# The head of a fused attention and mixture kernel: another written order, whole-tile conversions, more instructions ahead of the first scores

## The chip, the cores and the metric

The kernel runs on one core of a Trainium2 chip (trn2). The metric is the device time of one execution in microseconds (us). Engines are named as the profile names them: PE is TensorE, PEld its weight loads, DVE is VectorE, ACT is ScalarE, POOL is GpSimd, SP is SyncE, which issues the loads and stores.

## The reference

Three layers follow one another on 4 x 576 = 2304 tokens of width 512 (8 heads of 64). The first is attention, where a row sees only keys at a small distance (a window of 32 for heads 0 to 3; every fourth key of 128 for heads 4 to 7). The second is a gated layer, the third a mixture of 8 experts with 4 slots each.

```python
scores = np.where(masks, (q @ k.T) / np.sqrt(64), -1e9)
attn = np.exp(scores - scores.max(-1)); attn /= attn.sum(-1) + 1e-9
x = attn @ v                                     # 2304 x 512
x = (sigmoid(x @ w_gate) * (x @ w_val)) @ w_out  # 512 -> 1536 -> 512
logits = x @ phi                                 # 512 -> 32 slots
slot_input = softmax(logits, axis=0).T @ x       # 8 experts x 4 slots
slot_out[e] = relu(slot_input[e] @ w1[e]) @ w2[e]   # 512 -> 1024 -> 512
out = softmax(logits, axis=1) @ slot_out
```

## The kernel before

Tokens are worked on in five blocks: four of 512 and one of 256. In each block the 8 heads make four pairs, taken in the order `HP_ORDER`; a pair of a block is a *unit*. A unit passes these steps, each a function of the kernel:

- `scores`: on PE, two matmuls that add the mask (L146), then 32 products of q and k (L160), in fp32, which the trace lists as 64 matmuls and 64 weight loads. The result is in two PSUM tiles `s_ps`.
- `soft_max`: two maxima (L174) and two subtractions (L177) on DVE. `soft_exp`: ACT (L186). `soft_sum`: sum, a scalar addition, reciprocal on DVE (L191 to L193). `soft_norm`: the product with the reciprocal, on DVE or POOL (L197).
- `turn_unit`: four transposes on PE (L209), and a copy by ACT into `pt_ring` (L210).
- `sums` (by `weighted`, L236): 32 products of the turned probabilities and v, again 64 matmuls and 64 loads in the trace.
- `finish_unit`: the result is split into `x_hi` (ACT, L264) and `x_lo` (the difference, DVE, L265), so that a matmul in a faster format keeps precision.

The gated layer's first matmul (L485, `l1_chunk`) takes for each weight half and each unit three products: high weights by `x_hi`, high weights by `x_lo`, low weights by `x_hi`. The weights come in as 64-bit numbers in a tile `st` (`wd` in HBM). `convert_begin` orders that load; `convert_top` (ACT, L370), `convert_shift` and `convert_low` (DVE, L374 and L378) and `convert_sum` (POOL, L382) make 32-bit floats of them in `fw`, in two halves of 512 columns; `split_half` makes the high part `whl` (ACT, L442) and the low part (DVE, L443). `convert_end` notes the result to be stored.

`first_block` is the head of the program: the four units of the first block, the conversion of the weights z = 0 and z = 1, and the first L485 matmuls (`chunk`, six for each unit). Within it, `kept`, `kp` and `at` fix the order on each engine to the written one; behind it, a scheduler chooses. `keep_warm(n)` is n dummy matmuls on zeros (L110, 128 x 512, one weight load each), `pad_stream` is `PAD` short fp32 matmuls on data that is there (L873). `WARM` is the count of dummy matmuls at the start. `first_qk` and `first_v` order the loads of the second block, whose first instruction on PE is a mask matmul (L146). The lines of `first_block` from the second unit's exponentials to the fourth unit's turn are those that the change reorders.

Of the kernel before, what the change touches and what calls it, by code (L numbers as in the profile page):

```python
# [9 lines left out]
U32 = mybir.dt.uint32  # L10
# [16 lines left out]
WARM = 3  # L27
PAD = 8
# [24 lines left out]
def tile_kernel(  # L53
# [54 lines left out]
    def keep_warm(count):  # L108
        for _ in range(count):
            kept(nc.tensor.matmul(idle, lhsT=zero[:, 0:P], rhs=zero[:, 512:1024], start=True, stop=True))  # L110

    keep_warm(WARM)

# [71 lines left out]
    def soft_exp(u):  # L185
        kp(nc.scalar.activation(u["s"], u["s"], AF.Exp, scale=0.125))  # L186
# [172 lines left out]
    def convert_begin(z):  # L359
        i = n_conv[0]  # L360
        n_conv[0] += 1
        stage(z)
        if i + 1 < len(turn):
            stage(turn[i + 1])
        store()
        return b8(("ws", "ws", "gb", "xt")[i % 4] if i < NF else ("gb", "xt")[i % 2], [P, 2, 1024], F32, "fw")

    def convert_top(z, fw, h):
        c = slice(512 * h, 512 * h + 512)
        kp(nc.scalar.activation(fw[:, 0, c], staged[z][:, c, 1].bitcast(F32), AF.Prelu, scale=2.0**-112, alpha=2.0**32))  # L370

    def convert_shift(fw, h):
        top = fw[:, 0, 512 * h : 512 * h + 512].bitcast(U32)
        kp(nc.vector.tensor_scalar(top, top, 3, None, ALU.logical_shift_left))  # L374

    def convert_low(z, fw, h):
        c = slice(512 * h, 512 * h + 512)
        kp(nc.vector.tensor_scalar(fw[:, 1, c].bitcast(I32), staged[z][:, c, 0], 2.0**-29, None, ALU.mult))  # L378

    def convert_sum(fw, h):  # L380
        top, low = (fw[:, r, 512 * h : 512 * h + 512].bitcast(I32) for r in range(2))
        kp(nc.gpsimd.tensor_tensor(low, top, low, ALU.add))  # L382
# [10 lines left out]
    def convert(z):  # L393
        fw = convert_begin(z)
        for h in range(2):
            convert_top(z, fw, h)
            convert_shift(fw, h)
            convert_low(z, fw, h)
            convert_sum(fw, h)
        return convert_end(z, fw)  # L400
# [487 lines left out]
    def first_block():  # L888
# [10 lines left out]
        fw = [None, None]  # L899
        fw[0] = convert_begin(0)  # L900
# [9 lines left out]
        soft_norm(u[0], nc.gpsimd)  # L910
        scores(u[2], range(4))
        soft_max(u[2])
        soft_exp(u[2])
        soft_sum(u[1])
        soft_norm(u[1], nc.gpsimd)
        keep_warm(4)
        convert_top(0, fw[0], 0)
        turn_unit(u[0])
        convert_top(0, fw[0], 1)
        soft_sum(u[2])  # L920
        convert_low(0, fw[0], 0)
        convert_shift(fw[0], 0)
        convert_sum(fw[0], 0)
        soft_norm(u[2], nc.vector)
        convert_low(0, fw[0], 1)
        convert_shift(fw[0], 1)
        convert_sum(fw[0], 1)
        keep_warm(5)
        scores(u[3], range(4))
        turn_unit(u[1])  # L930
        soft_max(u[3])
        sums(u[0], u[2])
        finish_unit(u[0])
        soft_exp(u[3])
        whl = new_w()
        split_half(whl, fw[0][:, 1], 0, nc.vector)
        turn_unit(u[2])
        soft_sum(u[3])
        soft_norm(u[3], nc.vector)
        split_half(whl, fw[0][:, 1], 1, nc.vector)  # L940
        sums(u[1], u[3])
        finish_unit(u[1])
        convert_end(0, fw[0])
        first_qk()
        fw[1] = convert_begin(1)
        first_v()
        g = l1_tile(0, 0)
# [7 lines left out]
        turn_unit(u[3])  # L955
        for h in range(2):
            convert_top(1, fw[1], h)
            convert_low(1, fw[1], h)
            convert_shift(fw[1], h)
            convert_sum(fw[1], h)  # L960
        sums(u[2])
        finish_unit(u[2])
        chunk(HP_ORDER[1])
        sums(u[3])
        pad_stream(u[3])
        finish_unit(u[3])
        chunk(HP_ORDER[2])
        whl1 = new_w()
        for h in range(2):
            split_half(whl1, fw[1][:, 1], h, nc.vector)  # L970
        convert_end(1, fw[1])
# [508 lines left out]
```

## Time and profile before

| | before |
|---|---|
| median of three runs | 487.08 us (485.86 to 487.42) |
| the profiled execution's own time | 485.42 us |
| its span, first to last instruction | 483.6 us |
| PE busy | 463.6 us, 96% of the span |
| DVE, ACT, POOL busy | 308.4, 212.7, 156.8 us |
| instructions in the span | 12700 |

The profile is of one execution. A view by windows gives the busy time of each engine in a stretch and the clock granted to PE, where 1.00 is full speed; a timeline lists consecutive instructions of one kind with start and duration, and in brackets the idle time before them and what ended it. "issue" there means that nothing in the profile explains the wait. Since matmuls overlap, the start of the next instruction is often a better measure of a matmul than its duration.

### The profile page before, as it was taken

Reading aid. Unit: us, or ns where it says so; the run is one execution under the profiler, and the core shown is the slowest. Engines: PE = TensorE matmul, PEld = TensorE weight load, DVE = VectorE, ACT = ScalarE, POOL = GpSimd, SP = SyncE. Lnnn points to the kernel's source line nnn. Section 1 sums busy time; section 2 is a strip of 40 time slices with the busy share of each in tenths; the row PEclk is TensorE's granted clock in tenths of the full one; section 3 lists DMA queues with packets and bytes.
Section 4 is the critical chain, followed back from the end, with each engine's and each line's share of the span. In section 5 each row is a group of like instructions: output and inputs, shape, how many; then the busy total and the mean of one; then the engine's idle time right before and its main releaser. Section 6 shows DMA issues by size and latency. Waiting matters only on the chain.

```text
span 483.6 us, 12700 instructions
## 1 busy us (share of the span) xinstructions
PE 463.6 (96%) x5421; PEld 358.2 (74%) x5425; DVE 308.4 (64%) x627; ACT 212.7 (44%) x413; POOL 156.8 (32%) x134
## 2 busy tenths in 40 slices
PE   6799999999999999999999999999999999999993
PEld 3578877888778787787778888888887889842552
DVE  4877879848678666467776566656547765532623
ACT  2545455544446544445345545554535344300222
POOL 0334454425554663612033242333312124110100
PEclk9899999999999999999999999999999999999998
DMA  8979987986997792122220220211499886689966
GB/s 324 413 294 359 317 277 267 314 341 201 359 341 299 249 362 81 68 89 87 89 87 3 87 87 1 87 35 54 165 372 426 344 332 230 229 323 373 427 243 240
DMA packets 23720, 112.12 MB, mean 232 GB/s; under 512 B 2288, under 2 KB 7152, under 8 KB 14576
## 3 DMA queue, kind: packets, MB, share of 16 engines
q1 hardware_dynamic: 23664, 111.32, 61.8%
q8 instruction: 42, 0.69, 0.5%
q14 instruction: 14, 0.11, 0.1%
HBM read 97.16 MB, written 14.16 MB: 230 GB/s over the span
## 4 chain that ended last, share of the span: by engine, by line
PE 78%; DVE 4%; issue 1%; ACT 1%; POOL 1%; DVEq 0%; ACTq 0%; POOLq 0%
PE l1ps L485 25%; PE pa L610 13%; PE pe L610 7%; PE tp L743 4%; PE so_ps L1309 3%; PE pd L610 3%; PE h_ps L1247 3%; PE s_ps L236 3%; PE sp L768 2%; PE lt_ps L714 2%; PE s_ps L160 2%; PE wt_ps L419 1%; PE tr L209 1%; PE op L1347 1%; DVE whl L443 1%
## 5 line engine op out<-in xcount | busy, mean ns | idle before, releaser
L485 PE MATMUL l1ps<-x_hi,whl 128*128 128x512 f32 x384 | 130.6, 404 | 1.2 <-DVE g L471 1.0
L485 PEld LDWEIGHTS l1ps<-x_hi,whl 128*128 128x128 f32 x384 | 72.6, 189 | 18.1 <-DVE g L471 1.6
L485 PE MATMUL l1ps<-x_lo,whl 128*128 128x512 f32 x192 | 75.7, 394 | 0.0
L382 POOL TENSOR_TENSOR fw<-fw 128x512 int32<-128x512 int32 x36 | 47.8, 1337 | 55.9 <-DVE fw L374 24.7
L485 PEld LDWEIGHTS l1ps<-x_lo,whl 128*128 128x128 f32 x192 | 36.5, 190 | 6.3
L471 DVE SCALAR_TENSOR_TENSOR g<-g,l1ps 128x512 f32<-128x512 f32 (+1 forms) x36 | 21.4, 595 | 24.9 <-PE l1ps L485 24.8
L485 PE MATMUL l1ps<-x,whl 128*128 128x256 f32 x288 | 37.0, 285 | 0.0
L485 PEld LDWEIGHTS l1ps<-x,whl 128*128 128x128 f32 x288 | 35.4, 192 | 0.4 <-ACT whl L442 0.2
L443 POOL TENSOR_TENSOR whl<-w,whl 128x512 fp32r<-128x512 f32 x12 | 15.9, 1329 | 51.2 <-ACT whl L442 39.7
L497 ACT ACTIVATE g<-l1ps 128x512 f32<-128x512 f32 (+1 forms) x36 | 18.9, 526 | 30.3 <-PE l1ps L485 30.3
L443 DVE TENSOR_TENSOR whl<-fw,whl 128x512 fp32r<-128x512 f32 x24 | 21.8, 913 | 11.4 <-ACT whl L442 10.3
L442 ACT CAST whl<-fw 128x512 fp32r<-128x512 f32 x24 | 14.8, 622 | 26.6 <-POOL fw L382 26.5
L743 PEld LDWEIGHTS tp<-cst,g 128*128 128x128 f32 x192 | 21.3, 140 | 5.4 <-issue 4.1
L743 PE MATMUL tp<-cst,g 128*128 128x128 f32 x192 | 25.0, 275 | 0.0
L197 POOL TENSOR_TENSOR sm<-sm,su 128x512 f32<-128x512 f32 x14 | 17.3, 1237 | 23.7 <-DVE su L193 22.0
L370 ACT ACTIVATE fw<-st 128x512 f32<-128x512 f32 x36 | 22.8, 672 | 4.4 <-DMA st<-wd 4.4
L748 ACT COPY gt<-tp 128x512 f32<-128x512 f32 x24 | 14.0, 585 | 24.1 <-PE tp L743 21.4
L443 POOL TENSOR_TENSOR whl<-wst,whl 128x512 fp32r<-128x512 f32 x12 | 16.3, 1357 | 25.6 <-ACT whl L442 20.6
L673 DVE TENSOR_TENSOR tm<-pe,tm 128x512 f32<-128x512 f32 x12 | 8.3, 691 | 24.7 <-PE pe L610 24.7
L374 DVE TENSOR_SCALAR fw<-fw 128x512 uint32<-128x512 uint32 x36 | 20.5, 588 | 3.2 <-ACT fw L370 2.9
L236 PE MATMUL s_ps<-pt_ring,v 64*64 64x32 f32 (+1 forms) x992 | 18.9, 224 | 3.7 <-issue 3.7
L378 DVE TENSOR_SCALAR fw<-st 128x512 int32<-128x512 uint32 x36 | 18.2, 534 | 5.1 <-DMA st<-wd 4.9
(483 smaller groups left out, 954.3 us busy)
## 6 DMA issues: line engine op xcount, KB each, us to landing
ew<-w SPq DMA_DIRECT2D x32, 1024.0 KB, 7.5
st<-wd SPq DMA_DIRECT2D x18, 1024.0 KB, 7.9
wst<-wg SPq DMA_DIRECT2D x12, 1024.0 KB, 6.3
v<-qkv SPq DMA_DIRECT2D x20, 512.0 KB, 6.6
wg<-fw SPq DMA_DIRECT2D x12, 512.0 KB, 6.3
w<-wg SPq DMA_DIRECT2D x6, 1024.0 KB, 6.5
qk<-qkv SPq DMA_DIRECT2D x10, 576.0 KB, 5.1
qk<-qkv SPq DMA_DIRECT2D x8, 528.0 KB, 5.3
```

Of the source, the lines that this page charges most:

```text
L197: kp(norm.tensor_tensor(s, s, u["su"].unsqueeze(2).to_broadcast([P, 8, 64]), ALU.mult))
L236: nc.tensor.matmul(o, lhsT=v[k, t, i, r, :], rhs=p_[k, 2 * r + t, i, 0:nq], start=True, stop=True)
L370: kp(nc.scalar.activation(fw[:, 0, c], staged[z][:, c, 1].bitcast(F32), AF.Prelu, scale=2.0**-112, alpha=2.0**32))
L374: kp(nc.vector.tensor_scalar(top, top, 3, None, ALU.logical_shift_left))
L378: kp(nc.vector.tensor_scalar(fw[:, 1, c].bitcast(I32), staged[z][:, c, 0], 2.0**-29, None, ALU.mult))
L382: kp(nc.gpsimd.tensor_tensor(low, top, low, ALU.add))
L443: kp(eng.tensor_tensor(whl[:, 1, h], src[:, h], whl[:, 0, h].bitcast(F32), ALU.subtract))
L471: return nc.vector.scalar_tensor_tensor(g, g, 1.0, val, ALU.add, ALU.mult)
L485: nc.tensor.matmul(pt, lhsT=whl[:, w_, a, dc, :], rhs=x_[n][:, dc, :], start=(dc == HP_ORDER[0] and (w_, x_) == (0, x_hi)), stop=(dc == HP ...
L497: nc.scalar.activation(g, pt, AF.Tanh, scale=0.5)
L610: nc.tensor.matmul(pt, lhsT=w[:, w_, P * c : P * c + P], rhs=x_[:, c], start=first and c == 0 and w_ == 0 and x_ is hi, stop=c == 1 and w_ ...
L743: nc.tensor.transpose(tp[:, c], g_sb[self.n, 4 * q + c][:, P * j : P * j + P], ident)
```

## The change

It moves lines of `first_block` and changes three numbers:

- `WARM` from 3 to 7, and ahead of those, `SMALL` = 24 dummy matmuls of 32 x 32, each with its load: 28 matmuls and 28 loads more ahead of the first scores. `PAD` from 8 to 3. The dummy matmuls between the third and the fourth scores are 2, 2 and 3, in place of 4 and 5.
- In the head, `convert_top`, `convert_shift` and `convert_low` take the whole tile of 1024 columns at once; `convert_sum` keeps halves. Later conversions are as before.
- The second unit's sum and norm stand ahead of the third scores. The first and the second unit's turn both stand ahead of the fourth scores; before, the second one stood behind them.
- The fourth unit's exponentials, sum and norm stand ahead of `finish_unit` of the first unit; the third unit's turn behind that. The fourth unit's turn and the conversion of z = 1 stand ahead of the first `chunk`; the sums of the third and the fourth unit both stand between the first and the second `chunk`.

```diff
@@ -24,8 +24,9 @@
 HIP = 200
 LA = 2
 WO_AT = (12, 13, 14, 15, 16, 17)
-WARM = 3
-PAD = 8
+WARM = 7
+SMALL = 24
+PAD = 3
 GA = 0
 NRM = True
 ND = 4
@@ -109,6 +110,9 @@
         for _ in range(count):
             kept(nc.tensor.matmul(idle, lhsT=zero[:, 0:P], rhs=zero[:, 512:1024], start=True, stop=True))
 
+    for i in range(SMALL):
+        g = slice(32 * (i % 4), 32 * (i % 4) + 32)
+        kept(nc.tensor.matmul(idle[g, 0:32], lhsT=zero[:, 0:32], rhs=zero[:, 512:544], start=True, stop=True))
     keep_warm(WARM)
 
     def keep_busy(count):
@@ -365,20 +369,21 @@
         store()
         return b8(("ws", "ws", "gb", "xt")[i % 4] if i < NF else ("gb", "xt")[i % 2], [P, 2, 1024], F32, "fw")
 
-    def convert_top(z, fw, h):
-        c = slice(512 * h, 512 * h + 512)
+    HALVES = (slice(0, 512), slice(512, 1024))
+    WHOLE = slice(0, 1024)
+
+    def convert_top(z, fw, c):
         kp(nc.scalar.activation(fw[:, 0, c], staged[z][:, c, 1].bitcast(F32), AF.Prelu, scale=2.0**-112, alpha=2.0**32))
 
-    def convert_shift(fw, h):
-        top = fw[:, 0, 512 * h : 512 * h + 512].bitcast(U32)
+    def convert_shift(fw, c):
+        top = fw[:, 0, c].bitcast(U32)
         kp(nc.vector.tensor_scalar(top, top, 3, None, ALU.logical_shift_left))
 
-    def convert_low(z, fw, h):
-        c = slice(512 * h, 512 * h + 512)
+    def convert_low(z, fw, c):
         kp(nc.vector.tensor_scalar(fw[:, 1, c].bitcast(I32), staged[z][:, c, 0], 2.0**-29, None, ALU.mult))
 
-    def convert_sum(fw, h):
-        top, low = (fw[:, r, 512 * h : 512 * h + 512].bitcast(I32) for r in range(2))
+    def convert_sum(fw, c):
+        top, low = (fw[:, r, c].bitcast(I32) for r in range(2))
         kp(nc.gpsimd.tensor_tensor(low, top, low, ALU.add))
 
     def convert_end(z, fw):
@@ -392,11 +397,11 @@
 
     def convert(z):
         fw = convert_begin(z)
-        for h in range(2):
-            convert_top(z, fw, h)
-            convert_shift(fw, h)
-            convert_low(z, fw, h)
-            convert_sum(fw, h)
+        for c in HALVES:
+            convert_top(z, fw, c)
+            convert_shift(fw, c)
+            convert_low(z, fw, c)
+            convert_sum(fw, c)
         return convert_end(z, fw)
 
     ticks = [0]
@@ -896,8 +901,7 @@
         start_unit(u[3], "gb")
         for z in range(4):
             start_values(u, z)
-        fw = [None, None]
-        fw[0] = convert_begin(0)
+        fw = convert_begin(0)
         scores(u[0], range(4))
         soft_max(u[0])
         soft_exp(u[0])
@@ -908,42 +912,46 @@
         keep_warm(2)
         soft_sum(u[0])
         soft_norm(u[0], nc.gpsimd)
+        soft_sum(u[1])
+        soft_norm(u[1], nc.gpsimd)
+        convert_top(0, fw, WHOLE)
         scores(u[2], range(4))
         soft_max(u[2])
+        keep_warm(2)
+        turn_unit(u[0])
+        keep_warm(2)
+        turn_unit(u[1])
         soft_exp(u[2])
-        soft_sum(u[1])
-        soft_norm(u[1], nc.gpsimd)
-        keep_warm(4)
-        convert_top(0, fw[0], 0)
-        turn_unit(u[0])
-        convert_top(0, fw[0], 1)
+        convert_low(0, fw, WHOLE)
+        convert_shift(fw, WHOLE)
+        for c in HALVES:
+            convert_sum(fw, c)
         soft_sum(u[2])
-        convert_low(0, fw[0], 0)
-        convert_shift(fw[0], 0)
-        convert_sum(fw[0], 0)
         soft_norm(u[2], nc.vector)
-        convert_low(0, fw[0], 1)
-        convert_shift(fw[0], 1)
-        convert_sum(fw[0], 1)
-        keep_warm(5)
+        keep_warm(3)
         scores(u[3], range(4))
-        turn_unit(u[1])
         soft_max(u[3])
         sums(u[0], u[2])
-        finish_unit(u[0])
+        whl = new_w()
+        split_half(whl, fw[:, 1], 0, nc.vector)
         soft_exp(u[3])
-        whl = new_w()
-        split_half(whl, fw[0][:, 1], 0, nc.vector)
-        turn_unit(u[2])
         soft_sum(u[3])
         soft_norm(u[3], nc.vector)
-        split_half(whl, fw[0][:, 1], 1, nc.vector)
+        finish_unit(u[0])
+        turn_unit(u[2])
+        split_half(whl, fw[:, 1], 1, nc.vector)
         sums(u[1], u[3])
         finish_unit(u[1])
-        convert_end(0, fw[0])
+        convert_end(0, fw)
+        turn_unit(u[3])
         first_qk()
-        fw[1] = convert_begin(1)
+        fw = convert_begin(1)
         first_v()
+        convert_top(1, fw, WHOLE)
+        convert_low(1, fw, WHOLE)
+        convert_shift(fw, WHOLE)
+        for c in HALVES:
+            convert_sum(fw, c)
         g = l1_tile(0, 0)
         pt = [ps_l1.tile([P, 512], F32, tag="l1", name="l1ps") for _ in range(2)]
 
@@ -952,23 +960,17 @@
                 l1_chunk(0, whl, a, pt[a], dc)
 
         chunk(HP_ORDER[0])
-        turn_unit(u[3])
-        for h in range(2):
-            convert_top(1, fw[1], h)
-            convert_low(1, fw[1], h)
-            convert_shift(fw[1], h)
-            convert_sum(fw[1], h)
         sums(u[2])
         finish_unit(u[2])
-        chunk(HP_ORDER[1])
         sums(u[3])
         pad_stream(u[3])
         finish_unit(u[3])
+        chunk(HP_ORDER[1])
         chunk(HP_ORDER[2])
         whl1 = new_w()
         for h in range(2):
-            split_half(whl1, fw[1][:, 1], h, nc.vector)
-        convert_end(1, fw[1])
+            split_half(whl1, fw[:, 1], h, nc.vector)
+        convert_end(1, fw)
         chunk(HP_ORDER[3])
         for a in range(2):
             l1_gate(g, a, pt[a])
```

PE between the third scores (rows up to here: `s_ps_211`, `s_ps_212`) and the fourth (`s_ps_286`, `s_ps_287`), before; `idle<-pm` is a dummy matmul, `tr` a turn:

```order
L160 MATMUL s_ps_212<-qk 32x64
L110 LDWEIGHTS pm
L110 MATMUL idle<-pm 128x512
...
L209 MATMUL tr<-cst,sm_97 128x128 x4
...
L146 LDWEIGHTS msk
L146 MATMUL s_ps_286<-msk 128x256
```

The same place of the change, where the third scores are `s_ps_245` and `s_ps_246` and the fourth `s_ps_315` and `s_ps_316`:

```order
L164 MATMUL s_ps_246<-qk 32x64
L111 LDWEIGHTS pm
L111 MATMUL idle<-pm 128x512
...
L213 MATMUL tr<-cst,sm_125 128x128 x4
...
L213 MATMUL tr<-cst,sm_125 128x128 x4
...
L150 LDWEIGHTS msk
L150 MATMUL s_ps_315<-msk 128x256
```

Left out are only more dummy matmuls: four ahead of the turn and five behind it before, and now two, two and three. The second turn has come ahead of the fourth scores.

DVE from the third maxima to the fourth, before (`sm` are the probabilities of all units, `fw` and `st` the weights of z = 0; the L191 shown is the second unit's sum, the third's is left out up to its L193):

```order
L174 TENSOR_REDUCE mx<-s_ps_211 128x4
...
L177 TENSOR_TENSOR sm_97<-s_ps_212,mx 128x256
L191 TENSOR_REDUCE su<-sm_97 128x8
L192 TENSOR_SCALAR su<-su 128x8
...
L193 RECIPROCAL su<-su 128x8
L378 TENSOR_SCALAR fw<-st 128x512
L374 TENSOR_SCALAR fw<-fw 128x512
L197 TENSOR_TENSOR sm_97<-sm_97,su 128x512
L378 TENSOR_SCALAR fw<-st 128x512
L374 TENSOR_SCALAR fw<-fw 128x512
L174 TENSOR_REDUCE mx<-s_ps_286 128x4
```

And of the change, from the second unit's sum on:

```order
L195 TENSOR_REDUCE su<-sm_125 128x8
...
L197 RECIPROCAL su<-su 128x8
L178 TENSOR_REDUCE mx<-s_ps_245 128x4
...
L181 TENSOR_TENSOR sm_125<-s_ps_246,mx 128x256
L383 TENSOR_SCALAR fw<-st 128x1024
L380 TENSOR_SCALAR fw<-fw 128x1024
L195 TENSOR_REDUCE su<-sm_125 128x8
L196 TENSOR_SCALAR su<-su 128x8
L197 RECIPROCAL su<-su 128x8
L201 TENSOR_TENSOR sm_125<-sm_125,su 128x512
L178 TENSOR_REDUCE mx<-s_ps_315 128x4
```

The second unit's sum now stands ahead of the third maxima, and the conversions, each of the whole tile, ahead of the third unit's sum.

DVE from the fourth subtractions to the fourth norm, before (the first unit's `x_lo` is made from `s_ps_211` and `s_ps_212`):

```order
L177 TENSOR_TENSOR sm_97<-s_ps_287,mx 128x256
L265 TENSOR_TENSOR x_lo<-s_ps_211,x_hi 128x2x128
L265 TENSOR_TENSOR x_lo<-s_ps_212,x_hi 128x2x128
L443 TENSOR_TENSOR whl<-fw,whl 128x512
L191 TENSOR_REDUCE su<-sm_97 128x8
...
L193 RECIPROCAL su<-su 128x8
L197 TENSOR_TENSOR sm_97<-sm_97,su 128x512
L443 TENSOR_TENSOR whl<-fw,whl 128x512
L265 TENSOR_TENSOR x_lo<-s_ps_286,x_hi 128x2x128
```

And of the change:

```order
L181 TENSOR_TENSOR sm_125<-s_ps_316,mx 128x256
L448 TENSOR_TENSOR whl<-fw,whl 128x512
L195 TENSOR_REDUCE su<-sm_125 128x8
...
L197 RECIPROCAL su<-su 128x8
L201 TENSOR_TENSOR sm_125<-sm_125,su 128x512
L269 TENSOR_TENSOR x_lo<-s_ps_245,x_hi 128x2x128
L269 TENSOR_TENSOR x_lo<-s_ps_246,x_hi 128x2x128
L448 TENSOR_TENSOR whl<-fw,whl 128x512
L269 TENSOR_TENSOR x_lo<-s_ps_315,x_hi 128x2x128
```

The two differences for the first unit's `x_lo` have gone behind the fourth norm.

## Rows read from the trace of the kernel before

**Rows 1.** Page: span, busy time of each engine, instruction queue (packets, MB, share).
```profile
span 483.6 us, 12700 instructions
...
PE 463.6 (96%) x5421; PEld 358.2 (74%) x5425; DVE 308.4 (64%) x627; ACT 212.7 (44%) x413; POOL 156.8 (32%) x134
...
q8 instruction: 42, 0.69, 0.5%
```

**Rows 2.** Windows: stretch, length, busy us (instructions) by engine, clock, DMA share, GB/s.
```profile
0.00:34.00 34.00, 26.20 (x645) 18.67 (x652) 23.18 (x54) 14.11 (x28) 7.87 (x10) 0.90 0.92 360
```

**Rows 3.** Timeline of PE in the head: start, duration, instruction, idle before.
```profile
1.45 1.46 PE L110 MATMUL idle<-pm 128*128 128x512 bf16 x3 [1.45 <-DVE pm L101]
4.93 0.61 PE L146 MATMUL s_ps<-msk 128*128 128x256 bf16 x2 [2.01 <-DMA msk<-masks]
...
9.77 0.86 PE L160 MATMUL s_ps<-qk 64*32 64x64 f32 x64
...
12.45 0.66 PE L209 MATMUL tr<-cst,sm 128*128 128x128 f32 x4 [0.85 <-POOL sm L197]
...
15.71 1.13 PE L236 MATMUL s_ps<-pt_ring,v 64*64 64x32 f32 x63
19.50 0.19 PE L236 MATMUL s_ps<-pt_ring,v 64*64 64x32 f32 x1 [2.66 <-issue]
19.63 1.10 PE L209 MATMUL tr<-cst,sm 128*128 128x128 f32 x4
...
23.54 1.05 PE L485 MATMUL l1ps<-x_hi,whl 128*128 128x512 f32 x2
...
27.96 0.62 PE L485 MATMUL l1ps<-x_hi,whl 128*128 128x512 f32 x2
...
28.97 1.14 PE L236 MATMUL x_ps<-pt_ring,v 64*64 64x32 f32 x64
30.04 0.31 PE L873 MATMUL pad<-pt_ring,v 128*32 128x8 f32 x16
...
33.14 0.39 PE L146 MATMUL s_ps<-msk 128*128 128x256 bf16 x2
```

**Rows 4.** Windows on both sides of the clock's rise in the head.
```profile
19.83:26.66 6.83, 6.83 (x102) 5.42 (x101) 4.38 (x10) 3.27 (x8) 0.00 (x0) 0.51 1.01 396
26.66:33.10 6.44, 6.44 (x154) 5.20 (x146) 5.35 (x11) 4.08 (x10) 2.68 (x2) 1.00 0.85 322
```

**Rows 5.** Timelines of DVE and POOL (last three rows) in the head.
```profile
14.89 0.37 DVE L378 TENSOR_SCALAR fw<-st 128x512 int32<-128x512 uint32 x1
...
16.12 1.49 DVE L378 TENSOR_SCALAR fw<-st 128x512 int32<-128x512 uint32 x1
...
17.87 0.74 DVE L174 TENSOR_REDUCE mx<-s_ps 128x4 f32<-128x256 f32 x2
18.53 0.74 DVE L177 TENSOR_TENSOR sm<-s_ps,mx 128x256 f32<-128x256 f32 x2
...
21.77 0.68 DVE L191 TENSOR_REDUCE su<-sm 128x8 f32<-128x512 f32 x1
...
22.93 0.69 DVE L197 TENSOR_TENSOR sm<-sm,su 128x512 f32<-128x512 f32 x1
...
11.36 1.04 POOL L197 TENSOR_TENSOR sm<-sm,su 128x512 f32<-128x512 f32 x1 [10.91 <-DVE su L193]
...
15.68 1.65 POOL L382 TENSOR_TENSOR fw<-fw 128x512 int32<-128x512 int32 x1 [0.97 <-DVE fw L374]
18.02 1.26 POOL L382 TENSOR_TENSOR fw<-fw 128x512 int32<-128x512 int32 x1 [0.70 <-DVE fw L374]
```

**Rows 6.** Second hole: PE timeline, then window and instruction queue between the holes.
```profile
135.95 0.62 PE L485 MATMUL l1ps<-x_hi,whl 128*128 128x512 f32 x2
...
143.41 0.59 PE L236 MATMUL s_ps<-pt_ring,v 64*64 64x32 f32 x25 [1.04 <-issue]
...
19.40:143.30 123.90, 121.65 (x1910) 97.46 (x1909) 94.86 (x195) 63.45 (x122) 55.24 (x43) 0.97 0.86 309
...
q8 instruction: 15, 0.25, 0.8%
```

## The prediction

> **What bounds the kernel now.** Page and windows first: PE is busy 463.6 us of 483.6 [rows 1], and 26.20 of the first 34.00 [rows 2]. So 7.8 of its 20.0 idle microseconds lie in the head, and from 34.00 on it works 437.4 of 449.6: later work follows PE's instruction order with hardly a gap, and a microsecond that the head gains or loses moves all that follows. Then the PE timeline of the head [rows 3]. It shows four things. PE has nothing from 2.92 to 4.93, until the masks land (2.01). One matmul before the end of the first sums (x63, x1) it stands 2.66 us, released by "issue", that is by no engine and no data transfer. From 19.83 to 26.66 the granted clock is 0.51, that is 1.2 GHz of 2.4, and 1.00 behind that [rows 4], so two L485 matmuls take 1.05 there and 0.62 later, and a turn (four transposes) 1.10 against 0.66. And the head ends at 33.14, where the mask matmul of the second token block begins.
>
> What the third and fourth unit wait for is read from the VectorE and GpSimd timeline [rows 5]: the maxima of the fourth scores start at 17.87 although PE had those scores behind it when it began the sums at 15.71; VectorE is still converting weights (the low part at 16.12 took 1.49 against 0.37 for the same shape at 14.89, while GpSimd's add ran from 15.68 to 17.33).
>
> Last, the holes with no releaser. A second one, 1.04 us, lies at 143.41, 39 matmuls into a sums stretch [rows 6]. PE and its weight loads count 10846 instructions, the instruction queue 42 packets [rows 1]: 258 to a packet. Between the two holes lie 1910 + 1909 counted instructions and 15 instruction packets [rows 6]: 255 each. I read both holes as PE waiting for its next block of some 256 instructions. Both come at short instructions: a unit's sums are 128 of them (64 loads, 64 matmuls) in 1.13, so a whole block lasts some 2.3 us there.
>
> The Trainium skill (Runtime: NRT & Kernel Launch, Instruction fetch mechanics) has the same picture, blocks of 256 instructions, but calls a crossing "mostly hidden"; by that rule moving a border is worth nothing, which is rival D below. Most crossings here are indeed hidden, these two took 2.66 and 1.04.
>
> **The change, part by part.**
>
> *Start.* Seven first warm matmuls instead of three, and 24 small ones. Three take 1.46 at half clock [rows 3], so four more are some 1.8 (0.43 apart). Small ones: 16 pad matmuls took 0.31 [rows 3], 0.019 each, so 24 are 0.46; at half clock 0.9. Together 2.3 to 2.7 against a gap of 2.01: the first scores start 0.3 to 0.7 later. If the clock rises sooner, the first two units' masks (0.61 against 0.39 at 33.14) and the scores behind them shrink in the same ratio, by an estimated 0.3 to 0.5 for each unit. I take nothing: VectorE reaches the maxima of the third unit only at 12.6 (below), 2.0 behind the third scores' end (9.77 + 0.86), and that cover is worth those 2.0; it is lost only if the scores come later than that.
>
> *Order on VectorE until the fourth maxima.* Sum of the second unit goes ahead of the third maxima. Its scalar add must come between GpSimd's norm, which holds 11.36 to 12.40 [rows 5], so I let it end at 12.45 and the third maxima and subtractions run from 12.6 to 14.05 (0.74 + 0.74 less overlap, as at 17.87 to 19.27 [rows 5]). Whole-tile low and shift then: twice 0.37 and twice 0.42, 1.55, until 15.6. Two GpSimd adds start at once: 1.26 to 1.65 each [rows 5], until 18.2 at the lower price. The third unit's sum (0.68, as at 21.77) fits in front; its norm (0.69, both inputs in SBUF, as at 22.93) has to pass those two adds. If it slips in between them, the fourth maxima start at 18.0; if it waits for both, 18.2 + 0.7 + some 0.15 = 19.05. I take 19.05, as the low part at 16.12 was stretched for a whole add. So this point comes 1.2 *later* than before.
>
> *From the fourth maxima to the fourth norm.* Maxima and subtractions 1.40, one low half of the split 0.65 (of the norm's shape, 0.69 less overlap), sum to norm 1.85 (21.77 to 23.62): 22.95. Before it was 23.62, since from 19.27 to 21.77 lay not the half split alone but two x_lo differences of the first unit too, which waited for PE's late sums; those now follow. Gain at this point: 0.67. The first sums' hole falls away under this chain: the block border moves 56 - 4 = 52 instructions earlier, into the middle of the same 128-instruction sums, but until 22.95 PE has only two sums and a turn to do, and even 2.66 of waiting ends before.
>
> *From the fourth norm to the end of the head.* PE then has the last turn (0.5 of its 0.66 before the next can start), six L485 matmuls, two sums (28.97 to 30.04, 1.07 each), three pads in place of eight (0.1) and eighteen L485. Twelve L485 lie between the pad's end at 30.35 and the mask row: (33.14 - 30.35) / 12 = 0.233. So 0.5 + 24 x 0.233 + 2.14 + 0.1 = 8.3, and the head ends at 31.3: 1.8 earlier. That is at the full clock. At half clock, turn (1.10 - 0.66 = 0.44) and six matmuls (3 x (1.05 - 0.62) = 1.3) cost 1.7 more, and the head gains 0.1. What the clock will be depends on what PE does before: with only sums, turns and waits from about 16 to 22.95, as in the stretch that fell to 0.51 after the 2.66 hole, a fall is likely, but the two sums may keep it up for part. Between ends of 0.1 and 1.8 I take 0.9, the middle.
>
> The Trainium skill (TensorE: Matmul & The Clock Gate, Part 4: PE-mode transpose) says that transposes do not count as activity for the clock. By it, the three turns that now stand close together and ahead of the tail give the clock nothing, and the sum would be the half-clock one, 0.1 in the head. No row here separates a turn's part.
>
> *After the head.* The stream moves 56 - 4 - 20 = 32 instructions (pad: 5 matmuls fewer, 4 instructions each). The border that stops PE at 143.41 moves to 32 earlier in the same short instructions; but the border before it, from which on the next block can be fetched, lies among L485 matmuls as at 135.95 [rows 6] (0.233 for a load and a matmul, so 32 instructions are up to 3.7; counted in the trace, with the turns between them, about 2.6). The fetch starts 2.6 earlier, its use only some 0.3 earlier: 2.3 more lead than a hole of 1.04 needs. Gain 1.04; bounds 0 and 1.04. Other borders move as well, counting on in blocks of 256 to short stretches near 161 and 192; in before they were hidden, I take nothing, and up to 1.04 each against.
>
> *Sum.* 485.42 (the profiled run: span 483.6 and 1.8 around it) - 0.9 - 1.04 = 483.5. The profiled run lies 1.66 below the median of the runs, 487.08, so on that scale **485.1**.
>
> **The rivals.** The bound of what can be told from no change is 0.3%, 1.46 us.
>
> W, the clock stays up: 1.8 in the head and 1.04: 487.08 - 2.84 = 484.2. For it: more activity ahead of the scores, one hole shorter; against: PE still waits for the fourth norm.
>
> B, half clock in the tail: 0.1 + 1.04: 485.9, no measurable change. For it: the 0.51 of 19.83 to 26.66 [rows 4] came after a wait just like the one that now ends at 22.95.
>
> D, the second hole stays, or comes back at another border: only the head's 0.9: 486.2. For it: the moved borders near 161 and 192.
>
> C, slower. 52 instructions earlier, the border ahead of the first sums' one falls into the end of the third unit's scores, which before lay behind it in the warm matmuls at a wait. If PE stands there as at 19.50 (2.66) the scores end near 13.3, the third maxima start 0.7 late; if the fetch takes still longer, as transfers fill the queues (DMA share 0.92 [rows 2]), the whole 2.66 lies on the path, and with a hole of 1.04 at each of the two other borders it is 2.66 + 2.08 - 1.94 + 487.08 = 489.9. It decides from 3.4 us of new holes on (1.94 + 1.46). Against it: VectorE's later third maxima cover 2.0 of it.
>
> **How the numbers follow.** A (forecast) 0.36, its own range 484.4 to 485.9 (0.29 faster, 0.07 within 0.3%). W 0.18, faster. B 0.20 and D 0.09, same. C 0.17 (0.13 slower, 0.04 same, when only part of a hole shows). Faster 0.47, same 0.40, slower 0.13. The range takes in B, D, half of W's and the smaller half of C: 483.4 to 488.4.
>
> **What would show it.** Right: the maxima of the fourth scores at 19 and its norm near 23; the mask matmul of the second block at 31.5 to 33; no idle "issue" above half a microsecond in the sums near 142; a hole in the first sums with nothing late behind it. Wrong: fourth maxima at 18 or earlier, or behind 20; a hole of over 1.5 in the third unit's scores; new "issue" rows of about 1 at 161 or 192; granted clock 1.0 or 0.5 throughout the tail of the head, which decides between W and B.

## The result and the profile after

The change is slower: a median of 491.68 us over 13 runs (488.93 to 497.19) against 485.86 us over 13 runs of before (483.34 to 489.51); the ratio is 1.0108, 95% interval 1.0076 to 1.0140, that is 3.7 to 6.8 us. The forecast was 485.1 where before has 487.08, a ratio of 0.996. Runs more than 1.5% above the fastest of their kernel are left out of the ratios, among them one of the change (497.19) and the profiled one of before_small16 (493.24). The profiled execution of the change took 493.63, 8.2 more than that of before.

The page of the changed kernel, its span and busy times:

```profile
span 491.9 us, 12732 instructions
...
PE 469.8 (96%) x5441; PEld 361.7 (74%) x5441; DVE 310.5 (63%) x623; ACT 212.7 (43%) x411; POOL 156.8 (32%) x134
```

PE is busy 6.2 us longer [rows 1] although its work grew by 16 loads and about as many matmuls, most of them small: much of it is work at the lower clock. The timeline of PE in the head (start, duration, instruction, idle before it):

```profile
1.74 3.17 PE L111 MATMUL idle<-pm 128*128 128x512 bf16 x7
5.11 0.61 PE L150 MATMUL s_ps<-msk 128*128 128x256 bf16 x2 [0.20 <-DMA msk<-masks]
...
12.07 0.32 PE L164 MATMUL s_ps<-qk 64*32 64x64 f32 x9 [2.72 <-issue]
...
22.80 1.04 PE L213 MATMUL tr<-cst,sm 128*128 128x128 f32 x4 [1.51 <-DVE sm L201]
...
24.49 1.05 PE L490 MATMUL l1ps<-x_hi,whl 128*128 128x512 f32 x2
...
32.72 0.39 PE L150 MATMUL s_ps<-msk 128*128 128x256 bf16 x2
```

The seven warm matmuls end at 4.91, 0.2 ahead of the masks. The head ends at 32.72 in place of 33.14 [rows 3]. The hole at the end of the first sums is gone; one of 2.72 stands in the third scores, nine records before their end. The last turn begins at 22.80 and runs at half clock, as do the L490 matmuls behind it (1.05 for two). VectorE and ScalarE show what that tail waits for:

```profile
12.44 0.76 DVE L178 TENSOR_REDUCE mx<-s_ps 128x4 f32<-128x256 f32 x2 [0.50 <-PE s_ps L164]
...
15.70 0.58 ACT L214 COPY pt_ring<-tr 128x512 f32<-128x512 f32 x1 [1.12 <-PE tr L213]
16.18 0.63 ACT L190 ACTIVATE sm<-sm 128x512 f32<-128x512 f32 x1
16.92 0.69 DVE L195 TENSOR_REDUCE su<-sm 128x8 f32<-128x512 f32 x1 [1.86 <-ACT sm L190]
...
18.69 0.75 DVE L178 TENSOR_REDUCE mx<-s_ps 128x4 f32<-128x256 f32 x2
...
21.96 0.69 DVE L201 TENSOR_TENSOR sm<-sm,su 128x512 f32<-128x512 f32 x1
```

The third maxima start at 12.44, right behind the late scores, for which VectorE waits 0.50. The third unit's sum then waits 1.86 for its exponentials: ScalarE has them behind the copy of the second turn, and that turn came late from PE (1.12 of waiting at 15.70). The fourth maxima start at 18.69, and the fourth norm ends at 22.65 (23.62 before [rows 5]).

So the loss lies behind the head. Going through both traces by instruction, two places hold most of it. Of before, and then of the change, the rows are the mask matmul at the first of these places, the waits, the transposes of the output weights and the turn that frame the second, and the matmul behind the old hole (of the change also the mask and the sums ahead of the new one):

```profile
66.79 0.39 PE L146 MATMUL s_ps<-msk 128*128 128x256 bf16 x2
...
79.18 0.50 PE L485 MATMUL l1ps<-x_hi,whl 128*128 128x512 f32 x1 [1.02 <-DVE g L471]
...
133.63 0.66 PE L419 MATMUL wt_ps<-cst,fw 128*128 128x128 f32 x4
...
136.87 0.60 PE L209 MATMUL tr<-cst,sm 128*128 128x128 f32 x4
...
143.93 0.64 PE L425 MATMUL pt_ps<-pm,cst 128*32 128x256 f32 x8
```

```profile
66.10 0.47 PE L490 MATMUL l1ps<-x_hi,whl 128*128 128x512 f32 x1 [1.97 <-DVE g L476]
...
70.41 0.51 PE L150 MATMUL s_ps<-msk 128*128 128x256 bf16 x2
...
73.51 0.42 PE L240 MATMUL s_ps<-pt_ring,v 64*64 64x32 f32 x13 [0.87 <-issue]
...
134.86 0.39 PE L150 MATMUL s_ps<-msk 128*128 128x256 bf16 x2
...
135.97 1.12 PE L240 MATMUL s_ps<-pt_ring,v 64*64 64x32 f32 x61
139.56 0.42 PE L240 MATMUL s_ps<-pt_ring,v 64*64 64x32 f32 x3 [2.47 <-issue]
139.91 1.11 PE L424 MATMUL wt_ps<-cst,fw 128*128 128x128 f32 x4
...
145.86 0.60 PE L213 MATMUL tr<-cst,sm 128*128 128x128 f32 x4
...
151.65 0.64 PE L430 MATMUL pt_ps<-pm,cst 128*32 128x256 f32 x8
```

The mask matmul at 66.79 comes at 70.41: a lead of 0.42 has become a lag of 3.62. Some 0.65 of this shift of 4.04 is there by the mask matmul at 49.96 (49.73 before). In front of 66.10 PE waits 1.97 for VectorE's gate product, and from about 67.1 on it runs at half clock: twelve matmuls take 4.31 (66.10 to 70.41) where twelve at 0.233 take 2.8, so 1.5 more. The hole of 0.87 that follows is about made up by the 1.02 at 79.18 that before had. The matmul at 143.93 comes at 151.65, a lag of 7.72: a hole of 2.47 stands in the sums at 139.56, three records before their end, and the twelve matmuls and the transposes behind it take 5.95 (139.91 to 145.86) in place of 3.24 (133.63 to 136.87). The hole of 1.04 at 143.41 [rows 6] is gone. The span ends 8.3 later; 0.6 of lag comes at other places further on. Windows tell the clock (columns as in [rows 2]):

```profile
66.00:70.40 4.40, 4.30 (x12) 3.07 (x12) 1.95 (x2) 2.23 (x4) 0.70 (x1) 0.64 0.88 244
137.10:139.56 2.46, 0.00 (x0) 0.00 (x0) 1.19 (x4) 1.24 (x2) 0.27 (x2) 0.87 0.76 237
139.90:145.80 5.90, 5.90 (x17) 4.76 (x17) 3.62 (x8) 1.55 (x3) 2.10 (x2) 0.51 0.83 258
145.80:151.60 5.80, 5.80 (x151) 4.77 (x149) 2.81 (x4) 3.23 (x6) 2.30 (x2) 1.00 0.75 299
```

No matmul runs from 137.10 to 139.56; then the clock is 0.51 until 145.80, and 1.00 behind that. In the same stretch as the hole one packet of the instruction queue moves:

```profile
q8 instruction: 1, 0.02, 2.4%
```

The first of the two places is read on VectorE and GpSimd, before and then changed:

```profile
61.81 0.75 DVE L378 TENSOR_SCALAR fw<-st 128x512 int32<-128x512 uint32 x2
62.49 0.74 DVE L374 TENSOR_SCALAR fw<-fw 128x512 uint32<-128x512 uint32 x2
63.16 0.67 DVE L471 SCALAR_TENSOR_TENSOR g<-g,l1ps 128x512 f32<-128x512 f32 x1
```

```profile
62.87 0.41 DVE L383 TENSOR_SCALAR fw<-st 128x512 int32<-128x512 uint32 x1
63.20 0.75 DVE L380 TENSOR_SCALAR fw<-fw 128x512 uint32<-128x512 uint32 x2
63.87 1.48 DVE L383 TENSOR_SCALAR fw<-st 128x512 int32<-128x512 uint32 x1
65.28 0.67 DVE L476 SCALAR_TENSOR_TENSOR g<-g,l1ps 128x512 f32<-128x512 f32 x1
...
63.70 1.38 POOL L387 TENSOR_TENSOR fw<-fw 128x512 int32<-128x512 int32 x1 [1.30 <-DVE fw L380]
```

Before, two low parts, two shifts and the gate product (L471) follow one another without a delay. Now a low part stands between the shifts and the gate product. GpSimd's add starts at 63.70 as soon as the shift is done, the low part takes 1.48 in place of 0.41 until that add ends at 65.08, and the gate product starts at 65.28; PE waits for it until 66.10. That order was not written: behind the head the scheduler chooses, and it chose another order when the head had changed.

### The profile page after: what moved, and what is told of

It reads as the page before. It is cut to its first block, busy times and chain, and to the rows that moved or that the text cites. A ratio compares the mean times of both kernels' runs of the same rounds, so it can differ in the third digit from the quotient of the medians.

```text
span 491.9 us, 12732 instructions
## 1 busy us (share of the span) xinstructions
PE 469.8 (96%) x5441; PEld 361.7 (74%) x5441; DVE 310.5 (63%) x623; ACT 212.7 (43%) x411; POOL 156.8 (32%) x134
## 4 chain that ended last, share of the span: by engine, by line
PE 77%; DVE 4%; DMA 2%; ACT 2%; issue 1%; POOL 1%; ACTq 0%; DVEq 0%; POOLq 0%; SPq 0%
PE l1ps L490 25%; PE pa L615 13%; PE pe L615 6%; PE tp L748 4%; PE so_ps L1311 3%; PE pd L615 3%; PE h_ps L1249 3%; PE s_ps L240 3%; DMA w<-wg 2%; PE sp L773 2%; PE lt_ps L719 2%; PE s_ps L164 2%; PE wt_ps L424 1%; PE tr L213 1%; DVE whl L448 1%
## 5 line engine op out<-in xcount | busy, mean ns | idle before, releaser
L490 PE MATMUL l1ps<-x_hi,whl 128*128 128x512 f32 x384 | 133.2, 412 | 2.3 <-DVE g L476 2.0
L490 PEld LDWEIGHTS l1ps<-x_hi,whl 128*128 128x128 f32 x384 | 74.3, 194 | 19.8 <-ACT whl L447 2.4
L490 PE MATMUL l1ps<-x_lo,whl 128*128 128x512 f32 x192 | 77.2, 402 | 0.0
L490 PEld LDWEIGHTS l1ps<-x_lo,whl 128*128 128x128 f32 x192 | 37.3, 194 | 6.7
L490 PE MATMUL l1ps<-x,whl 128*128 128x256 f32 x288 | 37.3, 285 | 0.3 <-POOL whl L448 0.3
L490 PEld LDWEIGHTS l1ps<-x,whl 128*128 128x128 f32 x288 | 35.5, 191 | 0.9 <-POOL whl L448 0.5
L376 ACT ACTIVATE fw<-st 128x512 f32<-128x512 f32 (+1 forms) x34 | 22.4, 696 | 6.3 <-DMA st<-wd 6.3
L383 DVE TENSOR_SCALAR fw<-st 128x512 int32<-128x512 uint32 (+1 forms) x34 | 19.6, 598 | 4.5 <-DMA st<-wd 4.2
L380 DVE TENSOR_SCALAR fw<-fw 128x512 uint32<-128x512 uint32 (+1 forms) x34 | 20.5, 618 | 1.5 <-ACT fw L376 0.9
```

What stands on the lines that cost most here:

```text
L490: nc.tensor.matmul(pt, lhsT=whl[:, w_, a, dc, :], rhs=x_[n][:, dc, :], start=(dc == HP_ORDER[0] and (w_, x_) == (0, x_hi)), stop=(dc == HP ...
```

## The experiments

Two theories. **S, supply:** blocks of some 256 instructions arrive at PE; moved by 32, a border falls into the sums at 137 to 139, close behind the one before it, and the hole brings the half clock. **V, VectorE's order:** the scheduler's other order delays the gate product near 64, and that brings the half clock. They add if both hold. In the kernels below `SMALL` is the handle for S: it adds or takes instructions at the start, while the order on all other engines, and that on PE behind it, stays as it was (except where said). Each was timed in five rounds against the kernel before.

**small8**: the change, with

```diff
-SMALL = 24
+SMALL = 8
```

Expected: 

> The change with 8 small matmuls at the start in place of 24; every engine's order is that of the change, but all later instructions stand 32 earlier, so the instruction borders behind the head fall where they fell before. Theory S (the instruction supply): the 2.47 us hole at 137 and the half clock behind it (139.9 to 145.8) go and the old hole of about 1 us at 143 comes back, some 4 us less than the change, 487 to 488. Theory V (VectorE's order): the wait of 1.97 at 64 to 66 and the half clock behind it are all that counts and stay, 491 to 492. With both at work, the wait at 64 stays and the hole at 137 goes.

Measured: 1.0080 (1.0045 to 1.0114), median 489.09. Its PE rows behind the wait at 64, and behind the old hole:

```profile
65.84 0.47 PE L490 MATMUL l1ps<-x_hi,whl 128*128 128x512 f32 x1 [1.99 <-DVE g L476]
...
145.98 0.59 PE L240 MATMUL s_ps<-pt_ring,v 64*64 64x32 f32 x26 [0.20 <-issue]
```

No hole at 137; at the old place one of 0.20. The wait of 1.99 for the gate product stays. So the trace gives both theories a part; the times alone do not, since the 0.0028 between small8 and the change lies within their intervals.

**reorder_only**: the change, with

```diff
-WARM = 7
-SMALL = 24
-PAD = 3
+WARM = 3
+SMALL = 0
+PAD = 8
```

Expected: 

> The change's written order with the counts of before (3 warm matmuls, no small ones, 8 pads); instructions behind the head stand 4 earlier than before. Theory S: no hole at 137, one of about 1 us near 143, and the first-sums hole of 2.66 moves to the end of these sums or behind them; 486 to 488 by what the head gives. Theory V: a wait at VectorE's gate near 64 as in the change, 489 to 490; VectorE's order behind the head is neither that of before nor that of the change, so the wait may differ in size.

Measured: 1.0036 (1.0009 to 1.0063), median 487.47. In its trace there is no wait of 2 us near 64 (0.19 at 61.84, 0.76 at 79.67), none at 137, and 0.88 near 144; here the scheduler's order happens to be the good one. The head ends at 33.26, so in this execution the written order by itself wins nothing there. What brings the 1.0036, which is clear of 1, stays open.

**counts_only**: the kernel before, with `WARM = 7`, `PAD = 3` and the 24 small matmuls ahead of the warm ones:

```diff
+    for i in range(SMALL):
+        g = slice(32 * (i % 4), 32 * (i % 4) + 32)
+        kept(nc.tensor.matmul(idle[g, 0:32], lhsT=zero[:, 0:32], rhs=zero[:, 512:544], start=True, stop=True))
     keep_warm(WARM)
```

Expected: 

> The kernel before with 7 warm matmuls, 24 small ones and 3 pads; its written order is as before, instructions behind the head stand 36 later. Theory S: a hole of 2 to 2.7 in the sums near 134 to 137 with half clock behind it, and no hole at 143: about 4 more than before, 489 to 491. Theory V: no wait of 2 us at 64, the time of before within 1 us.

Measured: 1.0082 (1.0056 to 1.0108), median 490.08. So 56 instructions at the start and five pads fewer, with the written order of before, cost most of what the change costs. Not all is supply here: behind the head the scheduler moved a few instructions on VectorE, ScalarE and GpSimd, and the wait of 1.02 at 79.18 is 1.56 at 79.72. The trace has the hole:

```profile
136.44 0.30 PE L240 MATMUL s_ps<-pt_ring,v 64*64 64x32 f32 x4 [2.04 <-issue]
```

```profile
137.00:143.00 6.00, 6.00 (x33) 5.08 (x32) 5.53 (x10) 4.05 (x8) 3.81 (x3) 1.00 0.86 272
```

Here the clock stayed at 1.00 behind a hole of 2.04; this profiled execution (487.90) was the shortest of the kernel's runs. Behind the hole at this place the clock was 0.50 in before_small16 and in change_lows and 0.72 in reorder_small18, each over some 6 us.

**before_small16**: the kernel before with 16 of the small matmuls and nothing else; borders as in the change behind its head.

Expected: 

> The kernel before with 16 small matmuls at the start and nothing else: all orders are those of before, all borders lie 32 instructions earlier in the work, as in the change behind its head. Theory S: the hole of 2.5 near 134 to 137 with half clock behind it, none at 143: about 4 more than before less what the moved hole in the first sums gives back, 487 to 490. Theory V: the time of before within 1 us.

Measured: 1.0031 (1.0000 to 1.0062), with runs from 483.75 to 493.24. The hole stood at 137.37 with 2.35 in its trace, that of the longest run. The wide spread fits a hole behind which the clock falls in some executions only, and the mean clocks of the runs fit it too: 0.977 in the two longest, 0.989 to 0.997 in the three shortest. But the interval holds both theories' times; by itself this run decides nothing.

**reorder_small18**: reorder_only with `SMALL = 18`.

Expected: 

> The change's written order with 3 warm matmuls, 8 pads and 18 small matmuls: the orders of every engine are those of the run reorder_only, only the instructions behind the head stand 32 later than before, as in the change. Theory S (supply): the hole of about 2.5 in the sums near 137 comes back and the one at 143 goes, with half clock for some 6 us behind it where the clock falls: 489 to 491. Theory V (VectorE's order): no wait at 64, so the time of reorder_only, 487.5.

Measured: 1.0089 (1.0056 to 1.0123), median 489.06, against 1.0036 with no small matmuls.

```profile
137.24 0.30 PE L240 MATMUL s_ps<-pt_ring,v 64*64 64x32 f32 x3 [2.02 <-issue]
```

Thirty-six instructions that do nothing, ahead of everything, with every order the same: the hole is back at its place, with 2.02, and between 80 and 206 this execution takes 2.7 more than that of reorder_only. That is S without V. Another 1.65 of this execution stands at 432.43, where 24 matmuls (L1225) run at half clock and take 4.43 in place of 2.78, with no wait of PE ahead of them; the traces of before_small16 and reorder_small120 have this too, the others not, and no run explains it.

**reorder_small120** and **before_small120**: reorder_only and the kernel before with `WARM = 0` and `SMALL = 120`, borders 22 the other way.

Expected: 

> The change's written order with no warm matmuls, 120 small ones and 8 pads: orders as in reorder_only, all borders moved by 234 instructions, that is 22 the other way. By S no two borders stand within 5 us in the sums of the head or at 133 to 144, and the worst pair is one near 110 with at most 2 us: the hole near 143 goes, 485 to 487. By V no change against reorder_only, 487.5.

Expected: 

> The kernel before with no warm matmuls and 120 small ones at the start, orders else as before, borders moved by 234 instructions. By S the holes at 16.84 (2.66) and at 143 (1.04) both go, and with the first the half clock of 19.83 to 26.66; VectorE's chain to the fourth norm still holds PE, so of the 2.66 and some 3 of slow clock perhaps half is won: 482.5 to 485. If supply is not the cause of the holes, 486.

Measured: 1.0062 (1.0034 to 1.0091) and 1.0056 (1.0034 to 1.0078): both expectations missed. The hole near 143 stayed:

```profile
144.77 0.42 PE L240 MATMUL s_ps<-pt_ring,v 64*64 64x32 f32 x13 [0.79 <-issue]
```

```profile
145.39 0.43 PE L240 MATMUL s_ps<-pt_ring,v 64*64 64x32 f32 x14 [0.65 <-issue]
```

But it moved by the count. Before, 25 matmuls of these sums stood behind the hole [rows 6], now 14, and 13 in place of 24 in reorder_only: 11 matmuls with their loads are the 22 instructions. With the borders 32 earlier the hole at 137 has 2 or 3 matmuls behind it, in counts_only, with 36, it has 4. The place of the holes follows the instruction count, as S has it; their length does not follow from it. In before_small120 the head ended at 34.68: without the hole at 16.84 PE still waited 1.62 ahead of the second sums, and worked at half clock behind that, so that the time rose although a hole had gone. Moving borders the other way is no cure, and a rule of one fixed time from border to border does not place the holes.

**small8_lows**: small8, and in the later conversions the low parts written first:

```diff
         for c in HALVES:
+            convert_low(z, fw, c)
+        for c in HALVES:
             convert_top(z, fw, c)
             convert_shift(fw, c)
-            convert_low(z, fw, c)
             convert_sum(fw, c)
```

Expected: 

> The run small8 with the later conversions written with both low parts first; PE's and ScalarE's orders are those of small8, VectorE's differ so that no low part stands between a shift and the gate product near 64. Theory V: the wait of 2 us at 64 to 66 and the slow clock behind it go, 2.5 to 3.5 less than small8, 485.5 to 486.5. If the wait comes from elsewhere (the weights' load, the clock), it stays: 489.

Measured: 1.0022 (1.0004 to 1.0040), median 485.92, against 1.0080 for small8.

```profile
61.79 0.42 DVE L380 TENSOR_SCALAR fw<-fw 128x512 uint32<-128x512 uint32 x1
62.12 0.68 DVE L477 SCALAR_TENSOR_TENSOR g<-g,l1ps 128x512 f32<-128x512 f32 x1
62.72 1.12 DVE L380 TENSOR_SCALAR fw<-fw 128x512 uint32<-128x512 uint32 x1
```

```profile
62.94 0.47 PE L491 MATMUL l1ps<-x_hi,whl 128*128 128x512 f32 x1 [0.59 <-DVE g L477]
...
78.13 0.50 PE L491 MATMUL l1ps<-x_hi,whl 128*128 128x512 f32 x1 [1.24 <-DVE g L477]
```

The gate product now stands between the shifts, with no low part ahead of it, and PE waits 0.59 in place of 1.99; the next wait, at 78.13, is 1.24 in place of 0.49. Between the end of the head and 82 the trace of small8 takes 2.3 more than this one. V is shown, with the borders where they were, though for the order of all later conversions together: the edit moves instructions on VectorE at other places as well.

**change_lows**: the change with that edit alone.

Expected: 

> The change with only the later conversions rewritten (both low parts first): VectorE's order is that of the run small8_lows, borders stand as in the change. If supply and VectorE's order add up, the wait at 64 is gone and the hole of 2.5 near 137 with its slow clock stays: 2.5 to 4 above small8_lows, 488 to 489.5. If the hole needs the late VectorE work, it goes too: 486.

Measured: 1.0091 (1.0059 to 1.0123), median 490.79. The wait near 64 is 0.59, and the hole at 137.59 is 2.35:

```profile
65.22 0.47 PE L491 MATMUL l1ps<-x_hi,whl 128*128 128x512 f32 x1 [0.59 <-DVE g L477]
...
137.59 0.42 PE L240 MATMUL s_ps<-pt_ring,v 64*64 64x32 f32 x3 [2.35 <-issue]
```

S without V once more, and in the change's own order.

**lows_warm_tail** and **lows_warm_small0**: small8_lows with `SMALL = 4` (or 0) and

```diff
+        keep_warm(4)
         turn_unit(u[3])
         first_qk()
```

Expected: 

> The run small8_lows with four of its small matmuls taken from the start and four dummy matmuls of 128 x 512 put ahead of the fourth unit's turn, where PE waits 1.4 us for the fourth norm; all other orders and all later borders as in small8_lows. If the half clock in the tail of the head (seen in small8, not in small8_lows) is what a quiet stretch brings, it goes in every execution: 1 to 1.7 less in those where it fell, on the median about 0.8 less than small8_lows, 484.5 to 485.3. If the clock has another cause, the time of small8_lows, or 0.2 more if the dummies delay the turn.

Expected: 

> As lows_warm_tail with no small matmuls: borders 8 instructions the other way. If the hole of about 1 us near 143 shrinks as its border leaves the sums, up to 1 us less than lows_warm_tail; if the block's landing there is fixed by the full transfer queues, the same.

Measured: 0.9987 (0.9957 to 1.0016) and 1.0017 (0.9993 to 1.0042), both intervals overlapping that of small8_lows. In the trace of lows_warm_tail the clock had fallen ahead of the dummies and did not rise for them; in that of lows_warm_small0 it had not fallen, so the four tell nothing there. In the trace of lows_warm_tail the hole in the first sums is 2.58 and the clock behind it 0.52, in that of small8_lows, whose instructions up to there are the same but for four small matmuls, 0.70 and 1.00:

```profile
20.06 0.42 PE L240 MATMUL s_ps<-pt_ring,v 64*64 64x32 f32 x7 [2.58 <-issue]
```

```profile
20.00:24.00 4.00, 3.60 (x76) 3.08 (x77) 3.80 (x10) 2.74 (x7) 0.00 (x0) 0.52 1.03 417
```

```profile
18.71 0.42 PE L240 MATMUL s_ps<-pt_ring,v 64*64 64x32 f32 x11 [0.70 <-issue]
```

```profile
20.00:24.00 4.00, 2.58 (x66) 2.13 (x58) 3.80 (x11) 3.39 (x9) 0.00 (x0) 1.00 1.08 410
```

The head ends at 34.25 in the one and at 31.07 in the other; some 1.3 of that are the dummies themselves, which run at half clock from 23.72 to 25.00 with the fourth norm done. In lows_warm_small0 the hole near 143 was gone, and a new lag of 1.4 came near 406; it is as far from before as small8_lows.

**small4_lows**: small8_lows with `SMALL = 4`.

Expected: 

> The run small8_lows with 4 small matmuls in place of 8: all orders the same, borders 8 instructions the other way, as in lows_warm_small0, without its dummies ahead of the fourth turn. If the hole near 143 goes with the border (as the trace of lows_warm_small0 shows) and nothing else comes late, 0.5 to 1 less than small8_lows against the kernel before: ratio 0.998 to 1.001. If later waits take it back (as at 405 there), 1.002 as small8_lows.

Measured: 0.9986 (0.9962 to 1.0011), median 485.63 against 486.23: no difference from before that can be told. Its trace has the hole near 143 with 1.37, where lows_warm_small0 with the same border has none, so the ratio did not come by the way that was expected.

Together, on the change's order:

| | border as in the change | border as before (`SMALL = 8`) |
|---|---|---|
| scheduler's order as in the change | 1.0108 (after) | 1.0080 (small8) |
| low parts first | 1.0091 (change_lows) | 1.0022 (small8_lows) |

S is worth 0.0028 in the upper row and 0.0069 in the lower, 0.0048 in the mean, 2.4 us; V 0.0017 and 0.0058, 0.0038 in the mean, 1.8 us. By the intervals of the ratios each of these differences has 0.004 to 0.005 to either side (an estimate; each ratio was taken in its own group of runs against before). So 0.0069 and 0.0058 are clear of noise, 0.0028 and 0.0017 are not: from the change itself, taking away one of the two alone showed no measurable gain, taking away both did. Whether they add plainly can't be told. What is left, 0.0022, no run takes apart.

## Why the prediction was wrong

**The head: small in its gain, and the numbers on the way partly luck.** The first scores came 0.2 late (0.3 to 0.7 was said). The border fell into the third scores as rival C had it and cost 2.72. VectorE's third maxima were to cover it, and they came at 12.44 where 12.6 was worked out; but VectorE had been ready 0.50 earlier, and PE's late turns went on, by ScalarE, to the third unit's exponentials, which no step of the prediction had on the path. The fourth maxima at 18.69 are near the 19.05 that was said, by another way: the sum was to fit in ahead of GpSimd's two adds and the norm to wait for them, but the adds ran from 15.13 to 17.63, the sum came only at 16.92, and the norm (18.08) was not held up. In small8, whose instructions are the same but for 16 small matmuls, the third scores have no hole and the fourth maxima start at 18.18. The fourth norm ended at 22.65 (22.95), PE's turn began then, and the turn and six matmuls behind it ran at half clock: rival B's mechanism. Gain 0.42 where 0.9 was taken between 0.1 and 1.8. The reason given for 0.9, that the clock might hold in part, is in the runs a matter of the execution: the heads of small8_lows and small8 have the same instructions and ended at 31.07 and at 32.44, behind first-sums holes of 0.70 and 2.20.

**The old hole: right.** The lead that the shift gave the border closed the 1.04 at 143.41, here and in the four other kernels with the hole at 137. What it cost stood at the border before.

**The step that failed** is the sentence "Other borders move as well, counting on in blocks of 256 to short stretches near 161 and 192; in before they were hidden, I take nothing, and up to 1.04 each against." The border ahead of the old hole's was looked at only as the point from which the next block is fetched, not as a place where PE may wait itself; it had to move 2.6 us forward to give the lead. It moved out of the L485 matmuls into the end of the sums before them. Counted back from the hole stand 122 instructions of the sums (61 matmuls and their loads), 128 of the scores and 4 of the mask, some 254: about one block, which PE uses up in 2.2 us (134.86 to 137.09), and the next one came 2.47 after that. In the other kernels that hole measured 2.02, 2.35, 2.35 and 2.04 (reorder_small18, change_lows, before_small16, counts_only). The prediction counted the lead that the shift gave one border and not what it took from the border before. And it priced a hole at its length: the half clock behind it cost 2.7 more here, as the stretch from 19.83 to 26.66 [rows 4] had shown, and so the bound of 1.04 for each was far too low. Nothing happened at 161 or 192.

**What was left out altogether** is VectorE's order behind the head. The section on the work after the head moved PE's stream and let the other engines keep their order. The scheduler did not: it put a low part ahead of a gate product, beside GpSimd's add, 1.97 of waiting and 1.5 of half clock. The mechanism had been used in the head (the 1.49 at 16.12 [rows 5]) and was not looked for behind it. The Trainium skill (SBUF — State Buffer, SBUF: two separate sides) has VectorE and GpSimd share a port pair that one of them holds for a whole instruction; the low part at 63.87, which ends 0.27 behind GpSimd's add, agrees.

**Rival C** had the right sign with the wrong place: its hole in the third scores came and was covered but for some 0.5 (18.69 against 18.18 in small8), and what made the kernel slower was the same kind of hole 120 us later. Its price, 489.9 where before has 487.08, is a ratio of 1.0058, below the measured interval of 1.0076 to 1.0140.

**The rule on instruction supply** (the Trainium skill, Runtime: NRT & Kernel Launch, Instruction fetch mechanics: a crossing is "mostly hidden") does not hold in this kernel's short stretches: instructions added ahead of all work, with every order kept, brought 2.02 us of waiting at a place more than 100 us later (reorder_small18, with 1.0089 against 1.0036).

What stays open: why the same head has a first-sums hole of 0.70 in one execution (small8_lows) and of 2.20 in another (small8), why the clock held behind 2.04 in counts_only, and what the half clock near 432 in three traces comes from. How much the small waits at 47, 79 and 406 in several of the kernels add was not tried by itself.

## What to carry to other kernels

When an edit adds or removes instructions on a busy PE, list where all block borders go, not only the one that hurts now, and look for two that lie close together in time: a run of scores and sums, where a block lasts 2.2 us, is the place. Price a wait of 2 us by what the clock does behind it as well. When a scheduler orders what follows, compare the order on every engine to the end of the program: an edit of the head can move a product that PE waits for behind an operation that GpSimd's work stretches.

## What the runs showed of the hardware beyond that

Waits of PE of 0.70 and 0.84 in the first sums were followed by a clock of 1.00 (small8_lows, lows_warm_small0), those of 2.20 and 2.58 by 0.50 to 0.52 (small8, lows_warm_tail); a wait of 1.97 with PE busy on both sides was enough near 66, and one of 2.04 was not in counts_only. The length of the wait does not decide alone: the heads of the change and of change_lows have the same instructions, and behind the hole in the third scores (2.72 and 2.81) the clock was 0.66 from 12 to 17 in the change and 1.00 in change_lows:

```profile
12.00:17.00 5.00, 4.24 (x126) 3.24 (x127) 3.76 (x10) 2.88 (x5) 2.37 (x3) 1.00 1.03 418
```

Twenty-four matmuls of 32 x 32 with their loads took 0.35 us in the change, 0.0146 each: as a handle for moving borders they cost next to nothing while PE waits for the first masks anyway.
